# Local attention with a feed-forward gate: a reordered first quarter, and a planner that repairs modelled TensorE waits

## The chip, the cores and the metric

The kernel runs on one core of one Trainium2 chip. A core has five engines that run their own instruction streams side by side: TensorE (PE in the profile; its weight loads are listed as PEld), VectorE (DVE), ScalarE (ACT), GpSimd (POOL) and SyncE (SP), which issues most of the DMA transfers. The metric is the device time of one execution in microseconds; lower is better. It is given as the median of several runs.

## The reference

With x of 2048 tokens by 640 features, xn its layer norm, everything in float32:

```python
def _A_ref(x, wqkv, wo):          # x is xn here
    H = 32; Dh = D // H; W, dil = 8, 2
    qkv = (x @ wqkv).reshape(B, S, 3, H, Dh)          # q, k, v per head
    idx = pos[:, None] - (jnp.arange(W) * dil)[None, :]
    logits = einsum("bhsd,bhswd->bhsw", q, k[idx]) * Dh ** -0.5   # masked where idx < 0
    o = einsum("bhsw,bhswd->bhsd", softmax(logits), v[idx])
    return o.reshape(B, S, D) @ wo

def _B_ref(x, w1, w2):            # w1: 640 x 1536, w2: 1536 x 640
    return silu(x @ w1) @ w2

xn = layernorm(x)
return x + _A_ref(xn, wqkv, wo) * silu(_B_ref(xn, w1, w2))
```

Each token attends to eight tokens: itself and those 2, 4, ... 14 positions before it.

## The kernel before

**Groups and phases.** The 2048 tokens are cut into NG = 4 groups of 512 tokens, each of T = 4 tiles of 128. A group runs a q/k/v phase in NQ = 4 quarters of eight heads (480 columns of wqkv each), then the feed-forward phase with the output product of the group before woven in. The last output product ends the program.

**Two halves of every number.** Each float32 operand is split into a high part, rounded to TensorE's fast float32r format, and a residual low part. A product is three matmuls: high x high, low x high, high x low. For weights, line 479 (ACT) rounds a raw chunk into its high half `whi`, line 483 (GpSimd or VectorE) subtracts it from the raw chunk into the low half `wlo`, and for most chunks line 487 (SP) stores both for the later groups. For activations, TensorE transposes a piece, line 782 (ACT) copies it to `TH`, and line 786 (VectorE) subtracts into `TL`.

**The first quarter** (`first_quarter`, lines 745 to 838) is written out by hand, because nothing is loaded yet. TensorE first transposes the identity matrix WARM = 28 times, as dummy work (line 751). Each of the four token tiles is loaded into `XIN`, its statistics are taken by VectorE in two halves of 320 columns (line 764) and joined (765), ACT takes the root (526), VectorE the reciprocal (528), and VectorE normalizes it in two pieces (769). `PARTS` says how the five chunks of 128 columns are cut into the two pieces: three and two. `turn(t)` is the five transposes of tile t (778) with their copies (782) and residuals (786). `products(t, steps)` issues matmuls (799) for tile t; a step (k, c) is pass k on weight chunk c, with k = 0 high x high, 1 low x high, 2 high x low. A step (0, c) needs the rounded chunk, (2, c) its residual, (1, c) the activation's residual. The quarter has 4 tiles x 15 steps. The order of these calls is TensorE's order.

**Weight chunks in the first quarter.** The first RING = 7 chunks are loaded ahead (`raw_load`, 444 on SP, 440 on ACT for the chunk numbers in `BY_ACT`). Chunks 0 to 4 belong to the first quarter. Of the chunks below LO = 10, GpSimd subtracts the residual except for those in `ON_DVE`, (2, 3, 4), which VectorE does.

**The planner** (`Weave`). All work is first noted as operations with an engine, a modelled duration, keys that they read and write, and a priority. `order` then runs a model: each engine takes, among its operations whose inputs are there, the one that can start first, by priority among equals; TensorE keeps the order in which its work was noted. GpSimd's and VectorE's operations marked `lock` exclude each other in this model. The landing times of the first transfers are the constants `EARLY`, later ones follow a rate. The instructions are emitted in the order of their modelled starts. On the chip this fixes the order inside each engine and each DMA queue; between engines only real data dependences hold, by semaphores. So an order in the model between an operation of GpSimd and one of VectorE that share no data is not kept on the chip.

**Queues in the first microseconds.** SP issues the first half of tile 0, then chunk 0, tile 1 (`X_AT` = 3 for it, against priority 1 + k for chunk k), chunks 2, 3 and 4, tile 2, chunks 5 and 6, tile 3, and more chunks. ACT's queue takes the second half of tile 0 and chunk 1.

**The last quarter.** `o_rest` (730 to 742) transposes the last two chunks of the attention output of the last group (738, residual on VectorE at 742); VectorE's attention work before it is lines 680 to 720, its largest instructions being 680, 683 and 712.

Of the kernel before, what the change touches and what calls it, by code (L numbers as in the profile page):

```python
# [15 lines left out]
P = 128  # L16
# [40 lines left out]
TILE_AT = 1, 1.5, 5, 6  # L57
LOW_AT = 3
NOW = 3
ON_DVE = (2, 3, 4)  # L60


def win(ap, n, step):
# [10 lines left out]

class Op:
    __slots__ = ("eng", "dur", "fn", "prio", "lock", "table", "nbytes", "more", "late", "seq", "left", "users", "ready", "start", "end",
                 "spans")


class Weave:  # L80
# [19 lines left out]
    def add(self, eng, dur, fn, reads=(), writes=(), prio=0.0, lock=False, table=None, nbytes=0, more=0.0, late=0.0, at=0.0,  # L100
            spans=()):
        o = Op()
        o.eng, o.dur, o.fn, o.prio, o.lock, o.table, o.nbytes = eng, dur, fn, prio, lock, table, nbytes
        o.more, o.late, o.spans = more, late, spans
        o.seq, o.users, o.ready = len(self.ops), [], at
        before = set()
        for k in reads:
            if k in self.writer:
                before.add(self.writer[k])
        for k in writes:  # L110
            if k in self.writer:
                before.add(self.writer[k])
            before.update(self.readers.get(k, ()))
        for k in writes:
            self.writer[k] = o
            self.readers[k] = []
        for k in reads:
            self.readers.setdefault(k, []).append(o)
        before.discard(o)
        o.left = len(before)  # L120
        for b in before:
            b.users.append(o)
        self.ops.append(o)
        return o

    def order(self):
        engines = ("PE", "POOL", "DVE", "ACT", "SP")
        free = dict.fromkeys(engines, 0.0)
        can = {e: [] for e in engines}
        tensor = [o for o in self.ops if o.eng == "PE"]  # L130
        at = moved = 0
# [8 lines left out]
                        if a[0] == b[0] and a[1] < b[2] and b[1] < a[2] and (a[3] or b[3])), default=0.0)  # L140

        for o in self.ops:
            if o.left == 0:
                can[o.eng].append(o)
        done = []
        while len(done) < len(self.ops):
            best = None
            for e in engines:
                if e == "PE":
                    c = [tensor[at]] if at < len(tensor) and tensor[at].left == 0 else []  # L150
                else:
                    c = can[e]
                if not c:
                    continue
                f = free[e]
# [3 lines left out]
                if best is None or m < best[0] or (m == best[0] == lock and held == best[1].eng):  # L159
# [11 lines left out]
            o.start = t  # L171
            dur = o.dur
            if e == "ACT" and o.table is not None and o.table != table:
                table = o.table
# [2 lines left out]
            if o.nbytes:  # L177
                dma = max(dma, t + dur) + o.nbytes / self.RATE
                o.end = self.EARLY[moved] if moved < len(self.EARLY) else dma + self.LAND + o.more
                moved += 1  # L180
                lanes[e] = lanes[e][1:] + [o.end]
            else:
                o.end = t + dur
                if o.lock:
                    lock, held = o.end, e
            if e == "PE":
                at += 1
            else:
# [3 lines left out]
                live = [p for p in live if p.end > t - 30] + [o]  # L192
            for u in o.users:
                u.left -= 1
                u.ready = max(u.ready, o.end + (self.HOP + u.late if u.eng != e or o.nbytes else 0.0))
                if u.left == 0:
                    can[u.eng].append(u)
        self.span = max(o.end for o in done)
        return sorted(done, key=lambda o: (o.start, o.seq))

    def emit(self):
        for o in self.order():
            o.fn()


# [1 line left out]
def local_attention_silu_ffn(ctx: ExitStack, tc: tile.TileContext, x, wqkv, wo, w1, w2, out):  # L207
# [80 lines left out]
    po = lambda n: 0.11 + n * 0.0023  # L288

    def dve(n, fn, reads, writes, prio, lock=False, late=0.0, spans=()):  # L290
        add("DVE", dv(n), fn, reads, writes, prio, lock, late=late, spans=spans)

    def act(n, fn, reads, writes, prio, table=None, more=0.0, late=0.0, at=0.0, spans=()):
        add("ACT", ac(n) + more, fn, reads, writes, prio, table=table, late=late, at=at, spans=spans)

    def free_for(old, new):

# [95 lines left out]
        return QAT if i < first_q else 0  # L393

    raw_in = {}

    def raw_tile(k):

# [56 lines left out]
    def w_load():  # L455
# [19 lines left out]
        if not k:  # L475
            raw_load(0)
            rawn[0] = 1
        raw, kr = raws.pop(i)
        act(n, lambda: nc.scalar.activation(whi, raw, AF.Copy), kr + [("sd", 0)] * (k < 2), [kh], 1000 + due)
# [3 lines left out]
        add(eng, cost, lambda: by.tensor_tensor(out=wlo, in0=raw, in1=whi.bitcast(F32), op=OP.subtract),  # L483
            [kh] + kr + wait, [kl], due if pool_does else LOW_AT if k < LO else 50, lock=True)
# [38 lines left out]

    def ln_rstd(a, b, at=1):
        n = range(a, b)
        act(b - a, lambda: nc.scalar.activation(SD[:, 0, a:b], MV[:, a:b, 1], AF.Sqrt, bias=epst, scale=1.0),
            [("mv", t) for t in n], [("sd", t) for t in n], 0, "sqrt")
        dve(10, lambda: nc.vector.reciprocal(out=SD[:, 1, a:b], in_=SD[:, 0, a:b]),
            [("sd", t) for t in n], [("rs", t) for t in n], at)

    def ln_apply(t):
# [213 lines left out]
    def first_quarter(i):  # L745
# [3 lines left out]
        def warm(n, where):  # L749
            for k in range(n):  # L750
                nc.tensor.transpose(where[:, tsl(k % T)], ident, ident)
        pe(5.1, lambda: warm(WARM, ROT[0]), ["consts"], [("rot", 0)])

        PARTS = (0, 3), (3, DC)

        def begin(t):

# [2 lines left out]
            for k in range(2):  # L760
                cs = slice(k * 320, (k + 1) * 320)
                kx = ("xin", t) if t or k else ("xin", t, "a")
                turn_of = [("rs", t - 1)] if t == T - 1 else []
                dve(320, lambda k=k, cs=cs: nc.vector.bn_stats(out=st[:, k, :], in_=XIN[:, t, cs]), [kx] + turn_of, [ks + (k,)], at)  # L764
            dve(60, lambda: nc.vector.bn_aggr(out=MV[:, t, :], in_=st), [ks + (0,), ks + (1,)], [("mv", t)], -1)
            ln_rstd(t, t + 1, -1)
            for j, (a, b) in enumerate(PARTS):
                cs = slice(a * P, b * P)
                dve((b - a) * 64, lambda cs=cs: nc.vector.tensor_scalar(
                    out=XIN[:, t, cs], in0=XIN[:, t, cs], scalar1=MV[:, t, 0:1], scalar2=SD[:, 1, t:t + 1],  # L770
                    op0=OP.subtract, op1=OP.mult), [("rs", t), ("mv", t), ("xin", t)], [("xn", t, j)], at, lock=True)

        def turn(t):
# [5 lines left out]
                pe(0.11 * (b - a), go, [("xin", t), ("xn", t, j)], [kp])  # L779
            for a, b, j, tp, kp in parts:  # L780
                v = tp[:, :(b - a) * P].rearrange("p (c n) -> p c n", n=P)
                act((b - a) * P, lambda a=a, b=b, v=v: nc.scalar.activation(TH[i][:, a:b, tsl(t)], v, AF.Copy),
                    [kp], t_keys(i, range(a, b), [t], ["th"]), 0)
            for a, b, j, tp, kp in parts:
                v = tp[:, :(b - a) * P].rearrange("p (c n) -> p c n", n=P)
                dve((b - a) * P, lambda a=a, b=b, v=v: nc.vector.tensor_tensor(
                    out=TL[i][:, a:b, tsl(t)], in0=v, in1=TH[i][:, a:b, tsl(t)].bitcast(F32), op=OP.subtract),
                    [kp] + t_keys(i, range(a, b), [t], ["th"]), t_keys(i, range(a, b), [t], ["tl"]), 0)

# [46 lines left out]
        wv.writer["first"] = wv.ops[-1]  # L836
        w_done(DC)
        return ps
# [327 lines left out]
```

## Time and profile before

| | us |
|---|---|
| median of 3 runs | 627.77 (627.76 to 629.12) |
| the profiled execution: its span, first to last instruction | 625.9 |
| TensorE busy | 620.5 |
| VectorE busy | 543.9 |
| ScalarE busy | 264.6 |
| GpSimd busy | 110.8 |
| moved by DMA | 166 MB, mean 265 GB/s |

The profiled execution gives its span; the times of the runs also hold what lies around the span. "L799" is line 799 of the kernel. A row of the time line has the start, the length, the engine, the line, the operation, what it writes and reads, and the count of instructions merged in the row; in brackets stands the idle time before it and what ended it. TensorE's matmuls overlap, and their ends are modelled, so the distance of two starts says more than a matmul's length. A row of "groups by form" ends with busy us in total, mean ns of one instruction, and the idle time before them.

### The profile page before, as it was taken

How to read it: one execution, taken by the hardware profiler on the slowest of the kernel's cores; microseconds unless marked ns; L12 is line 12 of the kernel's file. 1: busy time of each engine (PE TensorE's matmuls, PEld its weight loads, DVE VectorE, ACT ScalarE, POOL GpSimd, SP SyncE). 2: the span in 40 equal slices, each digit the busy share in tenths (PEclk: the TensorE clock that was granted, in tenths of full speed). 3: DMA queues.
4: the chain of work that ended last, by engine and by line, in shares of the span. 5: the costliest groups of instructions: out<-in, count | busy, mean ns of one | idle time of the engine just before them, and what ended most of it. 6: DMA issues, size and time to landing. Idle time of an engine off the chain costs nothing.

```text
span 625.9 us, 9040 instructions
## 1 busy us (share of the span) xinstructions
PE 620.5 (99%) x3423; PEld 560.8 (90%) x3423; DVE 543.9 (87%) x548; ACT 264.6 (42%) x490; POOL 110.8 (18%) x159
## 2 busy tenths in 40 slices
PE   8999999999999999999999999999999999999997
PEld 7888899998889999999888998999988999999997
DVE  6599999999788988999969999999754999998934
ACT  5435556363536316353434504445644343252220
POOL 4500000011110142112221115211222211111100
PEclk9999999999999999999999999999999999999999
DMA  9999999499999999994899999999999999887662
GB/s 295 319 309 318 319 397 343 165 315 300 278 321 300 302 214 308 291 221 135 207 275 277 316 354 233 316 155 284 219 225 280 241 329 228 278 225 238 203 190 85
DMA packets 99260, 166.07 MB, mean 265 GB/s; under 512 B 31008, under 2 KB 60672, under 8 KB 99216
## 3 DMA queue, kind: packets, MB, share of 16 engines
q1 hardware_dynamic: 72720, 85.77, 53.1%
q0 software_dynamic: 25952, 79.31, 46.4%
q8 instruction: 27, 0.44, 0.3%
q10 hardware_dynamic: 544, 0.41, 0.2%
q14 instruction: 17, 0.14, 0.1%
HBM read 107.91 MB, written 34.16 MB: 227 GB/s over the span
## 4 chain that ended last, share of the span: by engine, by line
PE 98%; DMA 1%; DVE 0%; SPq 0%; issue 0%
PE acc L912 22%; PE acc L914 15%; PE acc L874 10%; PE acc L873 10%; PE acc L872 10%; PE rot L1038 9%; PE rot L1037 9%; PE rot L1036 9%; PE acc L799 2%; PE rot L542 1%; DMA xin<-in_A_x_dram 1%; PE rot L1022 0%; PE rot L778 0%; PE rot L738 0%; DVE st L764 0%; SPq L444 0%
## 5 line engine op out<-in xcount | busy, mean ns | idle before, releaser
L912 PE MATMUL acc<-w,sh 128*128 128x384 f32 x384 | 113.2, 334 | 0.0
L872 PE MATMUL acc<-w,th 128*128 128x512 f32 (+2 forms) x300 | 113.2, 377 | 0.0
L874 PE MATMUL acc<-w,th 128*128 128x512 f32 (+2 forms) x300 | 112.9, 376 | 0.0
L873 PE MATMUL acc<-w,tl 128*128 128x512 f32 (+2 forms) x300 | 112.8, 376 | 0.0
L914 PE MATMUL acc<-w,sh 128*128 128x256 f32 x384 | 107.1, 279 | 0.0
L680 DVE TENSOR_TENSOR pr<-q,kv 128x2560 f32<-128x2560 f32 x32 | 90.2, 2819 | 13.9 <-DMA kv<-kv 13.7
L1049 ACT ACTIVATE sh<-rot 128x512 fp32r<-128x512 f32 x48 | 28.8, 599 | 155.8 <-PE rot L1038 155.7
L1036 PE MATMUL rot<-th,w 128*128 128x512 f32 x240 | 94.4, 393 | 0.0
L1037 PE MATMUL rot<-tl,w 128*128 128x512 f32 x240 | 93.8, 391 | 0.0
L1038 PE MATMUL rot<-th,w 128*128 128x512 f32 x240 | 93.8, 391 | 0.0
L712 DVE TENSOR_TENSOR pr<-q,kv 128x2560 f32<-128x2560 f32 x32 | 90.3, 2822 | 0.7
L683 DVE TENSOR_REDUCE l<-pr 128x128 f32<-128x2560 f32 x32 | 90.0, 2813 | 0.2
L470 POOL DMA_DIRECT2D w<-half_q x52 | 37.4, 719 | 233.4 <-DMA xr<-in_A_wqkv_dram 93.0
L717 DVE TENSOR_TENSOR pr<-pr 128x1280 f32<-128x1280 f32 x64 | 75.4, 1179 | 1.3
L470 POOL DMA_DIRECT2D w<-half_w x72 | 38.6, 537 | 213.5 <-PE acc L914 98.2
L914 PEld LDWEIGHTS acc<-w,sh 128*128 128x128 f32 x384 | 72.2, 188 | 1.0
L912 PEld LDWEIGHTS acc<-w,sh 128*128 128x128 f32 x384 | 72.1, 188 | 1.0
L874 PEld LDWEIGHTS acc<-w,th 128*128 128x128 f32 x300 | 56.3, 188 | 8.7
L873 PEld LDWEIGHTS acc<-w,tl 128*128 128x128 f32 x300 | 56.3, 188 | 8.7
L872 PEld LDWEIGHTS acc<-w,th 128*128 128x128 f32 x300 | 56.3, 188 | 8.6
L912 PE MATMUL acc<-w,sl 128*128 128x384 f32 x192 | 57.8, 332 | 0.0
L639 ACT ACTIVATE kv<-acc 128x320 f32<-128x320 f32 x64 | 28.2, 440 | 68.7 <-PE acc L874 66.4
(115 smaller groups left out, 1036.0 us busy)
## 6 DMA issues: line engine op xcount, KB each, us to landing
w<-half_w POOLq DMA_DIRECT2D x72, 640.0 KB, 8.6
w<-half_q POOLq DMA_DIRECT2D x39, 512.0 KB, 5.6
half_w<-w SPq DMA_DIRECT2D x24, 640.0 KB
kv<-kv SPq DMA_DIRECT2D x16, 560.0 KB
kv<-kv SPq DMA_DIRECT2D x16, 420.0 KB
w<-half_wo POOLq DMA_DIRECT2D x10, 640.0 KB, 6.8
gate<-in_B_w_dram SPq DMA_DIRECT2D x16, 320.0 KB
w<-half_q POOLq DMA_DIRECT2D x13, 384.0 KB, 8.6
```

The source lines that it names most:

```text
L470: add("POOL", 1.0, lambda: nc.gpsimd.dma_start(both, src), [("half", u), ("half", u, "more")], [kh, kl], due + 10, nbytes=2 * n * P * 4)
L680: dve(2560, lambda t=t: nc.vector.tensor_tensor(out=PR, in0=win(qq[:, t:t + 2, :], W, 0), in1=win(kv[:, 0, t:t + 2, :], W, CQ), op=OP.mult ...
L683: dve(2560, lambda t=t: nc.vector.tensor_reduce(out=l[:, t:t + 2].rearrange("p t w h -> p (t w h)"), in_=PR.rearrange("p t w (h d) -> p (t ...
L712: dve(2560, lambda t=t, v=v: nc.vector.tensor_tensor(out=PR.rearrange("p t w (h d) -> p t (w h) d", d=DH), in0=e[:, t:t + 2].rearrange("p ...
L872: nc.tensor.matmul(o, hi, wh, start=c == 0, stop=False)
L873: nc.tensor.matmul(o, lo, wh, start=False, stop=False)
L874: nc.tensor.matmul(o, hi, wl, start=False, stop=c == DC - 1)
L912: nc.tensor.matmul(a[t][0][:, :CA], st, w[:, :CA], start=first, stop=last)
L914: nc.tensor.matmul(b[t // 2][0][:, h * CB:(h + 1) * CB], st, w[:, CA:], start=first and h == 0, stop=last, skip_group_check=True)
L1036: nc.tensor.matmul(h, wh[:, cs], TH[i][:, c, :], start=c == 0, stop=False)
L1037: nc.tensor.matmul(h, wh[:, cs], TL[i][:, c, :], start=False, stop=False)
L1038: nc.tensor.matmul(h, wl[:, cs], TH[i][:, c, :], start=False, stop=c == DC - 1)
```

## The change

*Constants.* WARM goes from 28 to 20. The first steps of tile 0 get a new order, with (2, 0) as the second. Chunk 0 in place of chunk 1 is loaded on ACT's queue; tile 1's load moves up to priority 1.2, ahead of chunk 1. `EARLY` gets other landing times. `ON_DVE` is gone, so GpSimd subtracts all ten residuals. `PARTS` becomes two chunks and three. The steps of the four tiles are interleaved in a new order, with tile 0's and tile 1's last (2, c) steps put later.

*Fixed orders.* `chain` makes each of a list of operations a predecessor of the next in the model. One list orders VectorE's work of the first quarter (statistics `st`, aggregate `ag`, reciprocal `rc`, normalization `ap`, residual `tl`, each with tile and piece), one ACT's (`sq` the root, `hi` the rounding of a chunk, `th` the copy of a transposed piece), and one puts GpSimd's residuals `lo` and three of VectorE's normalizations in turn.

*The repair.* `plan` runs the model, takes the first modelled wait of TensorE over 0.03 after model time 6, follows back what made it late (`blame`: operations that stood behind another one on their engine), tries for each such pair to put the late one first, keeps the one that moves the waiting TensorE work furthest forward, and goes on, up to 90 trials in all.

```diff
-WARM, WARM2 = 28, 3
+WARM, WARM2 = 20, 3
-FIRST = (0, 0), (0, 1), (1, 0), (1, 1), (0, 2), (1, 2), (0, 3), (1, 3), (0, 4), (1, 4)
-BY_ACT = (1,)
+FIRST = (0, 0), (2, 0), (1, 0), (0, 1), (1, 1), (0, 2), (1, 2)
+ON_VECTOR = (("st", 0, 0), ("st", 0, 1), ("ag", 0), ("rc", 0), ("ap", 0, 0), ("ap", 0, 1), ("st", 1, 0), ("st", 1, 1), ("tl", 0, 0),
+             ("ag", 1), ("tl", 0, 1), ("rc", 1), ("ap", 1, 0), ("ap", 1, 1), ("st", 2, 0), ("tl", 1, 0), ("tl", 1, 1), ("st", 2, 1),
+             ("ag", 2), ("rc", 2), ("ap", 2, 0), ("ap", 2, 1), ("st", 3, 0), ("st", 3, 1), ("tl", 2, 0), ("ag", 3), ("tl", 2, 1),
+             ("rc", 3), ("ap", 3, 0), ("ap", 3, 1))
+ON_SCALAR = (("sq", 0), ("hi", 0), ("th", 0, 0), ("th", 0, 1), ("hi", 1), ("sq", 1), ("hi", 2), ("hi", 3), ("th", 1, 0), ("th", 1, 1),
+             ("hi", 4))
+BY_ACT = (0,)
-X_AT = 3, 6, 8
+X_AT = 1.2, 6, 8
-LOW_AT = 3
-NOW = 3
-ON_DVE = (2, 3, 4)
...
-    EARLY = 3.9, 3.8, 4.9, 5.3, 6.05, 6.95, 7.7, 8.4, 9.4
+    EARLY = 4.1, 3.9, 5.5, 5.2, 6.5, 7.3, 8.1, 8.85, 9.7
+    TRIES = 90
...
+    def chain(self, *ops):
+        for a, b in zip(ops, ops[1:]):
+            a.users.append(b)
+            b.need += 1
...
+    def blame(self, o):
+        pairs, todo, seen = [], [(o, 0)], set()
+        while todo:
+            o, depth = todo.pop()
+            if o is None or o in seen or depth > 12 or (o.eng == "PE" and depth):
+                continue
+            seen.add(o)
+            b = o.behind
+            if o.eng != "PE" and b is not None and o.start > o.ready + 1e-6 and b.end > o.ready or o.nbytes and b is not None:
+                if b.eng != "PE":
+                    pairs.append((o, b))
+                todo.append((b, depth + 1))
+            if not (o.eng != "PE" and o.start > o.ready + 1e-6):
+                todo.append((o.why, depth + 1))
+        return pairs
...
+    def plan(self):
+        tensor = [o for o in self.ops if o.eng == "PE"]
+        self.next = {a: [b] for a, b in zip(tensor, tensor[1:])}
+        done = self.order()
+        left, given_up = self.TRIES, set()
+        while left > 0:
+            gap = next((o for o in self.gaps(done) if o not in given_up), None)
+            if gap is None:
+                break
+            was, found = gap.start, None
+            for a, b in self.blame(gap):
+                if self.reaches(b, a):
+                    continue
+                a.users.append(b)
+                b.need += 1
+                self.order()
+                left -= 1
+                a.users.pop()
+                b.need -= 1
+                if gap.start < was - 0.02 and (found is None or (gap.start, self.span) < found[:2]):
+                    found = gap.start, self.span, a, b
+            if found is None:
+                given_up.add(gap)
+            else:
+                self.chain(*found[2:])
+            done = self.order()
+        return done
...
     def emit(self):
-        for o in self.order():
+        for o in self.plan():
...
-        pool_does = k < LO and k not in ON_DVE
+        pool_does = k < LO
...
-        pe(5.1, lambda: warm(WARM, ROT[0]), ["consts"], [("rot", 0)])
-        PARTS = (0, 3), (3, DC)
+        pe(4.9, lambda: warm(WARM, ROT[0]), ["consts"], [("rot", 0)])
+        PARTS = (0, 2), (2, DC)
...
         products(0, FIRST)
         turn(1)
-        products(0, [(2, c) for c in range(NOW)])
-        products(1, passes(0, 1))
-        products(0, [(2, c) for c in range(NOW, DC)])
+        products(0, [(0, 3), (1, 3)])
+        products(1, [(0, 0), (0, 1), (0, 2), (0, 3), (1, 0), (1, 1)])
+        products(0, [(0, 4), (1, 4), (2, 1)])
+        products(1, [(0, 4), (1, 2), (1, 3), (1, 4), (2, 0), (2, 1)])
         turn(2)
-        products(1, passes(2))
+        for t in range(2):
+            products(t, [(2, 2)])
         products(2, passes(0, 1))
         turn(3)
-        products(2, passes(2))
+        for t in range(3):
+            products(t, [(2, 3)])
+        products(2, [(2, c) for c in range(3)])
+        for t in range(3):
+            products(t, [(2, 4)])
         products(3, passes(0, 1, 2))
+        wv.chain(*(head[k] for k in ON_VECTOR))
+        wv.chain(*(head[k] for k in ON_SCALAR))
+        wv.chain(head["lo", 0], head["ap", 1, 1], head["lo", 1], head["lo", 2], head["ap", 2, 1], head["lo", 3], head["ap", 3, 1],
+                 *(head["lo", k] for k in range(4, RING)))
```

More of the change, by code (lines that the diff above doesn't have):

```diff
@@ L76 @@
     __slots__ = ("eng", "dur", "fn", "prio", "lock", "table", "nbytes", "more", "late", "seq", "left", "users", "ready", "start", "end",
-                 "spans")
+                 "spans", "need", "at", "why", "behind")
 class Weave:
@@ L104, in add @@
         o.more, o.late, o.spans = more, late, spans
-        o.seq, o.users, o.ready = len(self.ops), [], at
+        o.seq, o.users, o.at, o.need = len(self.ops), [], at, 0
         before = set()
@@ L119, in add @@
         before.discard(o)
-        o.left = len(before)
+        self.ops.append(o)
         for b in before:
-            b.users.append(o)
-        self.ops.append(o)
-        return o
+            self.chain(b, o)
+        return o
+    def chain(self, *ops):
+        for a, b in zip(ops, ops[1:]):
+            a.users.append(b)
+            b.need += 1
     def order(self):
@@ L128, in order @@
         free = dict.fromkeys(engines, 0.0)
+        last = dict.fromkeys(engines)
         can = {e: [] for e in engines}
@@ L142, in order @@
         for o in self.ops:
+            o.left, o.ready, o.why = o.need, o.at, None
             if o.left == 0:
@@ L158, in order @@
                 m = min(est)
-                if best is None or m < best[0] or (m == best[0] == lock and held == best[1].eng):
+                if best is None or m < best[0] or (m == best[0] == lock and held is not None and held.eng == best[1].eng):
                     pick = min((o for o, t in zip(c, est) if t <= m + 1e-9), key=lambda o: (o.prio, o.seq))
@@ L171, in order @@
             o.start = t
+            o.behind = held if o.lock and held and held.end > free[e] else last[e]
+            last[e] = o
             dur = o.dur
@@ L184, in order @@
                 if o.lock:
-                    lock, held = o.end, e
+                    lock, held = o.end, o
             if e == "PE":
@@ L194, in order @@
                 u.left -= 1
-                u.ready = max(u.ready, o.end + (self.HOP + u.late if u.eng != e or o.nbytes else 0.0))
+                when = o.end + (self.HOP + u.late if u.eng != e or o.nbytes else 0.0)
+                if when > u.ready:
+                    u.ready, u.why = when, o
                 if u.left == 0:
@@ L199, in order, with reaches @@
         return sorted(done, key=lambda o: (o.start, o.seq))
+    def reaches(self, a, b):
+        seen, todo = {a}, [a]
+        while todo:
+            o = todo.pop()
+            if o is b:
+                return True
+            for u in o.users + self.next.get(o, []):
+                if u not in seen:
+                    seen.add(u)
+                    todo.append(u)
+        return False
+    def blame(self, o):
+        pairs, todo, seen = [], [(o, 0)], set()
+        while todo:
+            o, depth = todo.pop()
[10 more added lines that the diff above has]
+        return pairs
@@ new lines, in gaps @@
+    def gaps(self, done):
+        end = 0.0
+        for o in done:
+            if o.eng == "PE":
+                if o.start > max(end, self.FROM) + 0.03:
+                    yield o
+                end = o.end
+    FROM = 6.0
+    def plan(self):
[25 more added lines that the diff above has]
+        return done
@@ L290, in dve @@
     def dve(n, fn, reads, writes, prio, lock=False, late=0.0, spans=()):
-        add("DVE", dv(n), fn, reads, writes, prio, lock, late=late, spans=spans)
+        return add("DVE", dv(n), fn, reads, writes, prio, lock, late=late, spans=spans)
     def act(n, fn, reads, writes, prio, table=None, more=0.0, late=0.0, at=0.0, spans=()):
-        add("ACT", ac(n) + more, fn, reads, writes, prio, table=table, late=late, at=at, spans=spans)
+        return add("ACT", ac(n) + more, fn, reads, writes, prio, table=table, late=late, at=at, spans=spans)
     def free_for(old, new):
@@ L395, in local_attention_silu_ffn @@
     raw_in = {}
+    head = {}
     def raw_tile(k):
@@ L478, in w_load @@
         raw, kr = raws.pop(i)
-        act(n, lambda: nc.scalar.activation(whi, raw, AF.Copy), kr + [("sd", 0)] * (k < 2), [kh], 1000 + due)
-        pool_does = k < LO and k not in ON_DVE
+        head["hi", k] = act(n, lambda: nc.scalar.activation(whi, raw, AF.Copy), kr + [("sd", 0)] * (k < 2), [kh], 1000 + due)
+        pool_does = k < LO
         eng, cost, by = ("POOL", po(n), nc.gpsimd) if pool_does else ("DVE", dv(n), nc.vector)
         wait = [("xn", 0, 1)] if pool_does and k < DC else []
-        add(eng, cost, lambda: by.tensor_tensor(out=wlo, in0=raw, in1=whi.bitcast(F32), op=OP.subtract),
-            [kh] + kr + wait, [kl], due if pool_does else LOW_AT if k < LO else 50, lock=True)
+        head["lo", k] = add(eng, cost, lambda: by.tensor_tensor(out=wlo, in0=raw, in1=whi.bitcast(F32), op=OP.subtract),
+            [kh] + kr + wait, [kl], due if pool_does else 50, lock=True)
         if what[i] == "store":
```

14 lines of the change are left out of this document (7 added, 7 removed).

## The prediction

> **What bounds the kernel now.** First the page: span, busy time, and the engines' shares of the chain that ended last.
>
> ```profile
> span 625.9 us, 9040 instructions
> PE 620.5 (99%) x3423; PEld 560.8 (90%) x3423; DVE 543.9 (87%) x548; ACT 264.6 (42%) x490; POOL 110.8 (18%) x159
> PE 98%; DMA 1%; DVE 0%; SPq 0%; issue 0%
> ```
>
> TensorE is the bound. The profiled execution spans 625.9; the median of the runs shown is 627.77, so 1.9 lie around the span and I carry them unchanged. Next, where TensorE is not busy (windows: length, then busy time of PE, PEld, DVE, ACT, POOL, clock, DMA), and the list of what PE waited for:
>
> ```profile
> 6.85:23.40 16.55, 16.36 (x85) 13.27 (x84) 10.85 (x29) 10.21 (x27) 5.36 (x5) 1.00 1.09 368
> 23.40:590.00 566.60, 566.60 (x3099) 511.16 (x3099) 514.03 (x477) 245.84 (x448) 101.26 (x145) 1.00 1.04 271
> 590.00:600.00 10.00, 9.98 (x62) 9.01 (x62) 7.64 (x11) 3.37 (x6) 1.59 (x3) 1.00 0.60 198
> 622.00:625.90 3.90, 0.11 (x1) 0.00 (x0) 0.85 (x2) 0.00 (x0) 0.00 (x0) 0.76 0.24 84
> ...
> PE rot L751 <- POOL ident masks.py:199: 1.4, 1, 1.4
> ```
>
> From 23.4 to 590 there is no idle time at all, and 0.02 in the ten us behind. So repairing modelled TensorE waits there has nothing to win: the waits that the planner sees are not on the chip. What is left is the first 23.4 us and the 3.8 after the last matmul, which the diff does not touch. A matmul's end is modelled, so inside the first quarter I count starts, not busy time:
>
> ```profile
> 6.85 0.71 PE L778 MATMUL rot<-ident,xin 128*128 128x128 f32 x5
> 7.92 0.70 PE L799 MATMUL acc<-w,th 128*128 128x480 f32 x2
> ...
> 13.26 1.24 PE L799 MATMUL acc<-w,tl 128*128 128x480 f32 x5
> 14.78 0.71 PE L778 MATMUL rot<-ident,xin 128*128 128x128 f32 x5
> 15.24 2.41 PE L799 MATMUL acc<-w,th 128*128 128x480 f32 x10
> 17.49 1.24 PE L799 MATMUL acc<-w,tl 128*128 128x480 f32 x5
> ...
> 22.35 1.24 PE L799 MATMUL acc<-w,th 128*128 128x480 f32 x5
> 23.43 0.38 PE L872 MATMUL acc<-w,th 128*128 128x480 f32 x1
> L751 PE MATMUL rot<-ident x22: 421/421/476, 1.4 to 5.9; 128*128 128x128 f32 x22
> L751 PE MATMUL rot<-ident x28: 272/421/476, 1.4 to 6.7; 128*128 128x128 f32 x28
> ```
>
> A product costs (23.43-22.35)/5 = 0.216, a transpose (17.49-14.78-10x0.216)/5 = 0.11. The quarter has 60 products, 20 transposes and 3 dummies: 12.96+2.2+0.33 = 15.5. It takes 23.43-6.85 = 16.6, so 1.1 are waits, nearly all before 13.3: from there 42 products and 10 transposes need 9.07+1.1 = 10.17 and take 10.17. Ahead of it, 22 dummies start at 1.4 to 5.9, one per 4.5/21 = 0.214, at 421 ns; the last six come faster, at 272: the clock went up near 6.1.
>
> **The change, part by part.** These rows carry the prices (time line, then groups by form: busy, mean ns):
>
> ```profile
> 1.21 0.70 SPq L444 DMA_DIRECT2D pr<-in_A_wqkv_dram  x1
> 3.74 0.89 DVE L764 BATCH_NORM_STATS2 st<-xin 128x6 f32<-128x320 f32 x2 [2.29 <-DMA xin<-in_A_x_dram]
> 5.43 0.80 DVE L769 TENSOR_SCALAR xin<-xin,mv,sd 128x384 f32<-128x384 f32 x2
> 6.27 1.10 ACT L479 ACTIVATE w<-pr 128x480 fp32r<-128x480 f32 x2 [1.07 <-DMA pr<-in_A_wqkv_dram]
> 6.96 2.40 POOL L483 TENSOR_TENSOR w<-pr,w 128x480 fp32r<-128x480 f32 x2 [3.73 <-ACT w L479]
> 7.14 0.89 DVE L764 BATCH_NORM_STATS2 st<-xin 128x6 f32<-128x320 f32 x2 [0.91 <-DMA xin<-in_A_x_dram]
> 8.51 1.58 ACT L479 ACTIVATE w<-pr 128x480 fp32r<-128x480 f32 x3
> 9.04 0.86 DVE L769 TENSOR_SCALAR xin<-xin,mv,sd 128x384 f32<-128x384 f32 x2
> 9.82 1.78 DVE L483 TENSOR_TENSOR w<-pr,w 128x480 fp32r<-128x480 f32 x3
> 11.03 0.61 ACT L479 ACTIVATE w<-xr 128x480 fp32r<-128x480 f32 x1 [0.94 <-DMA xr<-in_A_wqkv_dram]
> 11.53 0.48 DVE L764 BATCH_NORM_STATS2 st<-xin 128x6 f32<-128x320 f32 x1
> 21.73 1.59 ACT L479 ACTIVATE w<-gate 128x480 fp32r<-128x480 f32 x3 [0.71 <-issue]
> ...
> L786 DVE TENSOR_TENSOR tl<-rot,th 128x384 fp32r<-128x384 f32 x4 | 2.2, 545 | 2.0 <-ACT th L782 1.9
> L769 DVE TENSOR_SCALAR xin<-xin,mv,sd 128x384 f32<-128x384 f32 x4 | 2.0, 492 | 0.1
> L786 DVE TENSOR_TENSOR tl<-rot,th 128x256 fp32r<-128x256 f32 x4 | 1.6, 410 | 0.0
> L769 DVE TENSOR_SCALAR xin<-xin,mv,sd 128x256 f32<-128x256 f32 x4 | 1.6, 405 | 0.0
> L765 DVE BATCH_NORM_AGGREGATE mv<-st 128x2 f32<-128x12 f32 x4 | 0.8, 209 | 0.1
> L526 ACT ACTIVATE sd<-mv,epst 128x1 f32<-128x1 f32 x4 | 1.2, 300 | 2.5 <-DVE mv L765 2.5
> L528 DVE RECIPROCAL sd<-sd 128x1 f32<-128x1 f32 x4 | 0.6, 162 | 0.7 <-ACT sd L526 0.7
> ```
>
> *Eight dummies fewer.* The 20th starts at 1.4+19x0.214 = 5.5 and is out of the way at 5.7. Tile 0's first normalized piece, now two chunks, is ready at 5.43+0.41 = 5.84. So the first transpose starts near 5.95 instead of 6.85: 0.9 gained, if what follows keeps up. Nothing else needed the dummies but the clock (a rival below).
>
> *Loads.* Weight chunk 0 goes to ACT's queue, which held chunk 1; on SP tile 1 moves up past one weight issue of 0.70, and chunk 1 falls behind it. Chunk 0 lands between 3.74 (tile 0, ahead of it on its queue) and 6.27 (its consumer now). I take 5.8, nearer the late end because tile 1 now shares the transfers with it. Its rounding (0.6) ends at 6.45, then come the copies of tile 0's transposes, then the first product near 7.05 instead of 7.92. The fixed order of ACT adds a wait here: both copies stand behind chunk 0's rounding, and PE behind them.
>
> *(2,0) as second product* waits for GpSimd: 6.45+1.2 = 7.7. All of PE stands behind it, with some 0.5 of the 0.9 lost again; but what is late next decides anyway.
>
> *Tile 1.* It lands between 6.27 (chunk 0, which held its place on SP) and 7.14; I take 6.5. Behind it on DVE: statistics 0.89, the first residual 0.41, aggregate 0.21, residual 0.55, reciprocal 0.16, both normalizations 0.9 less 0.1 of overlap: 9.5. Three transposes later, 9.9, PE has six products that need no more: 9.9+6x0.216 = 11.2.
>
> *Tile 2* must pass its first statistics on DVE before tile 1's first residual: in the fixed order of DVE, 0.48+0.41 after it lands. It lands after chunk 4 (the third of the three at 8.51, so by 9.5) and before the chunk rounded at 11.03, which stands behind it on SP: bounds 9.5 and 11.03, giving 10.4 to 11.9 for the residual; I take the middle, 11.2. Before, 11.53 came from DVE's three weight subtractions (1.78), which now go to GpSimd.
>
> *The rest of the quarter* from 11.2: 47 products and 10 transposes, 10.15+1.1 = 11.25, so it ends at 22.45. Tile 2's normalization is due on PE 11 products later, 13.6; DVE needs 0.55+0.48+0.21+0.3+0.16+0.8 = 2.5 and is done at 13.7: 0.1 lost. End 22.55 against 23.43: 0.9 gained. With tile 2's bounds, 0.2 to 1.4 (where tile 1 decides no later).
>
> *GpSimd.* All weight residuals of the quarter go there, 1.2 each, and the order "residual, normalization, residual" exists only in the planner: nothing on the chip makes GpSimd wait for DVE. The pair of normalizations at 9.04 ran beside GpSimd until 9.36 and took 0.86, against 0.80 for the pair at 5.43 without it. From that row a blocked pair costs 0.06; the other end is one residual, 1.2. I take 0.3 in all, nearer the row.
>
> The Trainium skill (SBUF — State Buffer, section "SBUF: two separate sides") says that GpSimd and a two-port DVE instruction hold one port pair by an exclusive lock, for the whole instruction. By that, the first normalization at 9.04 would have begun at 9.36 and the pair ended at 10.16; it ended at 9.90, so the row bears the rule out at most in part.
>
> *SP.* The stores of chunks 2 to 4 wait for GpSimd now, up to 2 us later, with the raw loads of the second quarter behind them on SP; those are rounded from 21.7 on, so this is covered. The planner's repairs after the quarter change orders on DVE, ACT, POOL and SP: taken as 0.
>
> Sum: -0.9+0.3 = -0.6; span 625.3, time 627.2.
>
> **The rivals.** *All waits go:* 5.95+15.5 = 21.45, 2.0 gained: 625.8. Against it: chunk and tile landings set the waits, and their order only shifts. *The loads land no earlier:* tile 1 at 7.14 makes 11.8, tile 2 late as well: 0.3 gained and lost to GpSimd, 627.8. For it: the three landings at 6.27, 7.14 and 11.03 follow each other under a full DMA (share 1.09). *GpSimd gets in front of both normalizations of tile 1:* 2x1.2 on the path that ends at 9.5, less 0.5 of slack against tile 2: -0.9+1.9 = +1.0, 628.8. That is the lock of the Trainium skill's SBUF — State Buffer at work, which the row at 9.04 shows at most in part.
>
> *The last quarter* is the one on the slower side. There DVE, not PE, is nearly late:
>
> ```profile
> L742 DVE TENSOR_TENSOR tl<-rot,th x2: 691/692/692, 594.6 to 596.6; 128x512 fp32r<-128x512 f32 x2
>   PEld rot L738: 0.4, 1
> L712 DVE TENSOR_TENSOR pr<-q,kv x32: 2812/2824/2827, 66.9 to 587.8; 128x2560 f32<-128x2560 f32 x32
> ```
>
> PE's transposes at L738 already wait for DVE's L742. If a repair puts one 2.82 product in front of what L742 needs, all of it falls on PE: 627.2+2.8 = 630.0. It decides as soon as DVE is over 0.02 later than now. Against it: a repair is kept only where the planner's own next wait moves forward.
>
> *The clock stays low.* If the shorter run of dummies kept PE at half rate for another stretch like 1.4 to 6.1 (4.7), some 4 us of work between 6 and 10.8 would take 8, with 1 us of waits to absorb it: +3, 630.2. Against it: transposes follow the dummies 0.25 later. The Trainium skill (TensorE: Matmul & The Clock Gate, part 1) has a free-running window of about 3.4 us of sustained activity; with that in place of 4.7 the price would be about 2, an estimate. The trace agrees as far as it goes: 4.7 from the first dummy to the faster pace lies between one such window and two.
>
> **How the numbers follow.** Forecast (gain of 0.2 to 1.4) 0.52; loads no earlier 0.15; GpSimd 0.14; all waits gone 0.06; last quarter 0.09; clock 0.04. The measurement of this kernel tells 0.3%, 1.9 us, from no change. Only "all waits gone" reaches that bound on the fast side: faster 0.06. The last two and the tail of GpSimd's make slower 0.14. The rest, 0.80, is same. The forecast's own range is 626.4 (1.4 gained, nothing lost to GpSimd) to 627.9 (0.2 gained); the range to 8 in 10 takes in the loads and GpSimd: 625.8 to 629.4.
>
> **What would show it.** First real transpose near 5.95; first product near 7; tile 1's first statistics before 7.14; the first L872 near 22.5; no PE wait from there to 590. Wrong if the first L872 is later than 23.4, if a normalization in the quarter takes over 1 us, or if PE shows waits after the quarter.

## The result and the profile after

| kernel | median us | runs | span of the profiled execution |
|---|---|---|---|
| before | 627.82 (627.58 to 629.12) | 8 | 625.9 |
| changed | 629.61 (629.28 to 630.71) | 8 | 627.5 |

The changed kernel takes 1.0028 of the time before, with a 95% interval of 1.0018 to 1.0038: 1.8 us slower, 0.2 above the upper end of the predicted range. Here and below, medians and ratios leave out the few runs in the chip's slower state, and a ratio is not that of the two medians shown, because it also weighs some runs of before of 630 to 636 us (for e5, further down, the medians alone give 0.9985, the ratio 0.9958).

The page of the changed kernel, span, busy time and the chain that ended last:

```profile
span 627.5 us, 9020 instructions
PE 620.1 (99%) x3415; PEld 559.4 (89%) x3415; DVE 548.2 (87%) x545; ACT 264.9 (42%) x490; POOL 116.2 (19%) x162
PE 97%; DVE 1%; ACT 1%; DMA 0%; issue 0%
```

The windows that were shown of before (length, then busy time of PE, PEld, DVE, ACT, POOL, clock, DMA), and what PE waited for:

```profile
6.85:23.40 16.55, 14.63 (x71) 11.18 (x70) 13.71 (x31) 8.54 (x23) 7.95 (x7) 1.00 0.96 305
23.40:590.00 566.60, 566.60 (x3099) 511.13 (x3098) 513.30 (x471) 247.38 (x451) 103.45 (x145) 1.00 1.01 272
590.00:600.00 10.00, 9.98 (x59) 8.76 (x58) 8.02 (x9) 2.69 (x5) 1.20 (x3) 1.00 0.68 217
...
PE rot L863 <- DVE xin L854: 1.9, 3, 0.8
```

Behind the first quarter all is as before: from its end to the end of the span it is 602.6 us, against 602.5 (625.9-23.43). Inside it TensorE now idles 1.92 of 16.55 us where it was 0.19, and it waits for VectorE's normalization (L854, which was L769). The time line of PE in the first quarter of the changed kernel:

```profile
5.91 0.94 PE L863 MATMUL rot<-ident,xin 128*128 128x128 f32 x5 [0.19 <-DVE xin L854]
6.92 1.07 PE L884 MATMUL acc<-w,th 128*128 128x480 f32 x2
...
9.37 0.44 PE L863 MATMUL rot<-ident,xin 128*128 128x128 f32 x2
10.64 0.55 PE L863 MATMUL rot<-ident,xin 128*128 128x128 f32 x3 [0.84 <-DVE xin L854]
...
14.91 0.44 PE L863 MATMUL rot<-ident,xin 128*128 128x128 f32 x2
16.19 0.55 PE L863 MATMUL rot<-ident,xin 128*128 128x128 f32 x3 [0.84 <-DVE xin L854]
...
24.92 0.38 PE L967 MATMUL acc<-w,th 128*128 128x480 f32 x1
```

The start came as predicted: first transpose 5.91, first product 6.92, 0.9 and 1.0 earlier. Then, in tile 1 and again in tile 2, two transposes run and the other three stand 1.27 and 1.28 after them. The quarter ends at 24.92 instead of 23.43: 1.5 later, of the 1.6 by which the span grew. What VectorE and GpSimd did at the first of these places, single instructions of the changed kernel:

```profile
7.94 1.23 POOL L568 TENSOR_TENSOR w<-pr,w 128x480 fp32r<-128x480 f32 x1 [0.48 <-ACT w L564]
8.28 1.04 DVE L854 TENSOR_SCALAR xin<-xin,mv,sd 128x256 f32<-128x256 f32 x1
9.12 1.25 POOL L568 TENSOR_TENSOR w<-pr,w 128x480 fp32r<-128x480 f32 x1
9.24 1.35 DVE L854 TENSOR_SCALAR xin<-xin,mv,sd 128x384 f32<-128x384 f32 x1
10.33 1.33 POOL L568 TENSOR_TENSOR w<-pr,w 128x480 fp32r<-128x480 f32 x1
10.51 0.48 DVE L849 BATCH_NORM_STATS2 st<-xin 128x6 f32<-128x320 f32 x1
10.91 0.40 DVE L871 TENSOR_TENSOR tl<-rot,th 128x256 fp32r<-128x256 f32 x1
```

Each normalization starts on time and its row only grows longer; no idle time is shown. The first ends at 9.32, 0.15 after the GpSimd residual that was running (7.94+1.23 = 9.17). By then GpSimd's next residual is under way, and the second normalization ends at 10.59, 0.22 after that one (9.12+1.25 = 10.37). The statistics at 10.51 and the residual from PSUM at 10.91 run beside GpSimd at their usual 0.48 and 0.40. So it is not VectorE as a whole that GpSimd holds up, but the normalization. Tile 2 repeats it:

```profile
13.48 2.44 POOL L568 TENSOR_TENSOR w<-xr,w 128x480 fp32r<-128x480 f32 x2
...
13.62 2.52 DVE L854 TENSOR_SCALAR xin<-xin,mv,sd 128x256 f32<-128x256 f32 x2
```

The pair takes 2.52 and ends at 16.14, 0.22 after GpSimd's second (15.92). The planner's order, "residual, normalization, residual", holds in its model alone. On the chip GpSimd runs its residuals as soon as their chunks are rounded.

### The profile page after: what moved, and what is told of

Same layout as the page of the kernel before. It is cut to its first block, busy times and chain, and to the rows that moved or that the text cites. A ratio compares the mean times of both kernels' runs of the same rounds, so it can differ in the third digit from the quotient of the medians.

```text
span 627.5 us, 9020 instructions
## 1 busy us (share of the span) xinstructions
PE 620.1 (99%) x3415; PEld 559.4 (89%) x3415; DVE 548.2 (87%) x545; ACT 264.9 (42%) x490; POOL 116.2 (19%) x162
## 4 chain that ended last, share of the span: by engine, by line
PE 97%; DVE 1%; ACT 1%; DMA 0%; issue 0%
PE acc L1007 22%; PE acc L1009 15%; PE acc L969 10%; PE acc L968 10%; PE acc L967 10%; PE rot L1132 9%; PE rot L1133 9%; PE rot L1131 9%; PE acc L884 1%; PE rot L627 1%; DVE xin L854 1%; DMA xin<-in_A_x_dram 0%; PE rot L863 0%; ACT w L564 0%; PE rot L1117 0%; PE rot L823 0%
## 5 line engine op out<-in xcount | busy, mean ns | idle before, releaser
L802 DVE TENSOR_TENSOR pr<-pr 128x1280 f32<-128x1280 f32 x64 | 77.1, 1205 | 1.4
```

The lines of the kernel that those rows point to most:

```text
L802: dve(2 * n * CQ, lambda n=n: nc.vector.tensor_tensor(out=PR[:, :, 0:n, :], in0=PR[:, :, 0:n, :], in1=PR[:, :, n:2 * n, :], op=OP.add), [] ...
```

## The experiments

The times of before are those measured on the same chip beside each kernel.

| run | what it is | median us | before | ratio, 95% interval |
|---|---|---|---|---|
| e1 | changed, GpSimd held | 630.16 | 627.59 | 1.0038, 1.0015 to 1.0060 |
| e2 | changed, no repair | 633.92 | 627.59 | 1.0090, 1.0066 to 1.0114 |
| e3 | before, all residuals on GpSimd | 632.41 | 627.59 | 1.0065, 1.0018 to 1.0112 |
| e4 | before, repair alone | 628.16 | 627.59 | 1.0017, 0.9983 to 1.0052 |
| e5 | as e1, its tile last in SBUF | 626.81 | 627.74 | 0.9958, 0.9924 to 0.9992 |
| e6 | before, four unused bytes | 630.82 | 627.74 | 1.0048, 1.0019 to 1.0077 |
| e7 | e5 with 28 dummies | 630.98 | 627.74 | 1.0040, 1.0011 to 1.0069 |
| e8 | e5 with the loads of before | 632.02 | 627.74 | 1.0050, 1.0022 to 1.0078 |
| e9 | as e7, orders of e5 | 627.07 | 627.84 | 0.9977, 0.9954 to 1.0000 |
| e10 | changed, three residuals back on VectorE | 634.44 | 627.84 | 1.0095, 1.0061 to 1.0129 |

**e1: the planner's order made real.** A one-column sum on GpSimd reads the end of a normalized tile, so that GpSimd really waits for it.

```diff
     epst, SD = small("epst", 1), small("sd", 2, T)
+    HELD = small("held", 1)
...
+        for t, k in ((1, 1), (2, 3), (3, 4)):
+            last = XIN[:, t, D - 1:D]
+            o = add("POOL", po(1), lambda last=last: nc.gpsimd.tensor_tensor(out=HELD, in0=last, in1=last, op=OP.add),
+                    [("xn", t, 1), ("xin", t)], [("held",)], 0)
+            wv.chain(head["ap", t, 1], o, head["lo", k])
         wv.writer["first"] = wv.ops[-1]
```

> Changed kernel, with GpSimd made to wait on the chip for what only the planner's order says: a one-column sum of tile 1, 2 and 3 after their second normalization stands in front of the residuals of chunks 1, 3 and 4. Theory (GpSimd's residuals stood in front of four normalizations, 1.0 us lost for tile 1 and 1.0 for tile 2): the pairs of normalizations take 0.8 to 0.9 instead of 2.31 and 2.52, the quarter ends near 22.9 instead of 24.92, time 629.6 - 2.0 = 627.6. Rival (the repairs, the loads or the missing dummies cost the time): the pairs get short, but the time stays over 629.

The quarter did what the theory says: it ended at 22.38, 2.5 before the changed kernel, and no normalization took over 0.48. The time did not follow, 630.16: over 629, as the rival had it, though for none of its reasons, as e5 and e6 will show. No row shows a new wait of TensorE. Between 23 and 620 us the products themselves had become slower. Products of line 912 (here L1013) in the groups by form, busy us and mean ns, of before, then of e1:

```profile
L912 PE MATMUL acc<-w,sh 128*128 128x384 f32 x384 | 113.2, 334 | 0.0
```

```profile
22.38 0.38 PE L973 MATMUL acc<-w,th 128*128 128x480 f32 x1
...
L1013 PE MATMUL acc<-w,sh 128*128 128x384 f32 x384 | 115.2, 338 | 0.0
```

The 384-column products from sl went the same way, from a mean of 332 to 338, and those of 256 columns from 279 to 280.

The tile for the sum, four bytes per partition, stood ahead of the tiles sh, sl and others, so the addresses behind it had moved. That became a theory of its own, for e5 and e6.

**e2: the changed kernel without the repair.**

```diff
-        for o in self.plan():
+        for o in self.order():
```

> Changed kernel without the repair: the planner's first order is emitted. Theory: the repair has no part in the loss; the quarter ends between 24.5 and 25.3, no TensorE wait behind it, time 629.2 to 630.0. Rival (the repair's swaps made the loss): 627.8 or below.

633.92, against the theory and against its rival. The loss in the quarter is the same (it ended at 25.03, and PE waited 2.2 for L854), so the repair did not make it. But without the repair three waits stand later that neither before nor the changed kernel has. PE's waits in e2:

```profile
PE rot L863 <- DVE xin L854: 2.2, 3, 0.8
PE acc L1007 <- DVE sl L1146: 1.4, 1, 1.4
...
PE rot L823 <- DVE o L805: 1.3, 1, 1.3
PE acc L967 <- ACT gate L1220: 1.1, 1, 1.1
```

These three add up to 3.8 of the 4.3 between this kernel and the changed one. The new first quarter shifts the plan of all that follows, the planner's first order of it is late at three places, and the repair mends all three.

**e3: more GpSimd residuals in the kernel before.**

```diff
-ON_DVE = (2, 3, 4)
+ON_DVE = ()
```

> Kernel before with one edit: the residuals of chunks 2, 3 and 4 go to GpSimd as well. Theory: GpSimd runs five residuals back to back from 7.0 to 13.2, so two to four normalizations of tiles 1 and 2 last 1.0 to 1.4 instead of 0.4 to 0.5, and the first quarter ends 0.5 to 2 later: 628.3 to 629.8. Rival (the port is not the cause): 627.8, or faster, because VectorE has 1.8 less to do.

The theory's mark is there, one normalization of 1.36 and a wait of 2.0 behind it, but the time is far over its range. The five residuals of GpSimd, that normalization, the waits, and a window of e3:

```profile
6.97 6.06 POOL L483 TENSOR_TENSOR w<-pr,w 128x480 fp32r<-128x480 f32 x5 [3.74 <-ACT w L479]
...
11.82 1.36 DVE L769 TENSOR_SCALAR xin<-xin,mv,sd 128x256 f32<-128x256 f32 x1
...
PE rot L1036 <- DMA w<-half_w: 2.8, 1, 2.8
PE rot L778 <- DVE xin L769: 2.0, 1, 2.0
PE rot L738 <- DVE o L720: 1.3, 1, 1.3
...
13.90:17.20 3.30, 3.30 (x9) 2.66 (x9) 2.73 (x9) 0.49 (x2) 1.52 (x2) 0.50 1.10 383
```

GpSimd ended at 13.03 and this normalization, one of 256 columns, at 13.18: again 0.15 later. The wait of 2.0 was followed by a stretch at half clock (0.50), nine matmuls in 3.3 us, and the other plan brought two later waits, 2.8 and 1.3. The quarter ended at 27.00, 3.6 later than before. One edit, four prices: only the first was in the expectation.

**e4: the repair alone on the kernel before** (its `plan`, `blame` and `chain`, landing constants as before).

> Kernel before with the repair alone, first quarter and landing constants as before. Theory: TensorE's waits in the model are not on the chip; 627.8 within 0.4. Rival (the repairs shift work on VectorE that TensorE needs): over 628.5, with new waits of TensorE in the profile.

628.16, the interval holds 1: no gain to be seen. A small loss is likely, for all ten runs (from 627.78) lie above the median of before, and the rival's mark is there in small. TensorE waits 0.3 for tile 1's second normalization, which now starts at 11.16, behind a weight residual of VectorE at 10.59; in the kernel before the two normalizations ran as a pair. The quarter ended 0.4 later than before, at 23.80:

```profile
23.80 0.38 PE L953 MATMUL acc<-w,th 128*128 128x480 f32 x1
```

**e5: e1 with the tile behind all others.**

```diff
-    HELD = small("held", 1)
...
     TURN = sb.tile([P, TOK], F32, name="turn")
+    HELD = small("held", 1)
```

> As the held kernel (GpSimd really waits for tiles 1, 2 and 3), but the one-column tile lies behind all others in SBUF instead of ahead of the operand tiles. Theory (the first quarter gained 2.4 us there against the changed kernel, and the shifted addresses of the operand tiles gave 3.1 back through slower products): no shift now, the first quarter ends near 22.5, the mean of the 128x384 products from sh is 334 again, time 627.6 - 0.8 = 626.8, between 626.3 and 627.3. Rival (the drift came from the wait itself or from the later schedule): 630 again.

As the theory has it: 626.81, 0.9 below before. Against the changed kernel that is 2.7, each taken against before on its own chip. It is the fastest of all here, and its slowest run (627.12) is faster than the fastest run of before beside it (627.22). Its normalizations (x8 is their count; then shortest, median and longest ns), GpSimd's wait, and the end of the quarter:

```profile
L855 DVE TENSOR_SCALAR xin<-xin,mv,sd x8: 411/444/476, 5.6 to 16.2; 128x256 f32<-128x256 f32 x4, 128x384 f32<-128x384 f32 x4
...
9.73 0.19 POOL L934 TENSOR_TENSOR held<-xin 128x1 f32<-128x1 f32 x1 [2.17 <-DVE xin L855]
9.88 2.40 POOL L569 TENSOR_TENSOR w<-pr,w 128x480 fp32r<-128x480 f32 x2
...
22.83 0.38 PE L973 MATMUL acc<-w,th 128*128 128x480 f32 x1
```

No normalization is over 476 ns. GpSimd idles 2.17 and starts after the pair. The quarter ends 2.1 before that of the changed kernel, and what follows it takes 602.5, as before.

**e6: nothing but four bytes.**

```diff
     epst, SD = small("epst", 1), small("sd", 2, T)
+    PAD = small("pad", 1)
```

> Kernel before with one edit: an unused tile of four bytes per partition where the held kernel had its own, ahead of sh, sl and what follows. Theory (addresses): the first quarter is as before, the mean of the 128x384 products from sh goes from 334 to 338, time 627.6 + 3.1 = 630.7. Rival (addresses play no part): 627.6.

630.82: an unused tile in the kernel before costs 3.1, with the same group means as in e1 (busy us, mean ns; the 256-column group has 280 again). The first quarter, which ended at 23.27, has no part in it:

```profile
L913 PE MATMUL acc<-w,sh 128*128 128x384 f32 x384 | 115.2, 338 | 0.0
```

Which of the shifted tiles matters, and to which multiple it has to lie, was not tried.

**e7 and e9: the dummies.** Both are e5 with WARM = 28. In e7 the planner also counts them as 28 (5.1), in e9 as 20 (4.9), so that the other engines run e5's orders unchanged.

> The held kernel (tile last) with 28 dummy transposes instead of 20. Theory: the first real transpose is back at 6.85, 0.9 later; of that, what tile 1's chain does not absorb shows at the end of the quarter: 0.2 to 0.9 over the held kernel, 627.0 to 627.7. Rival (the dummies are worth nothing, tile 1 decides): as the held kernel.

> The held kernel (tile last) with 28 dummy transposes, but with the modelled time of 20, so that VectorE, ScalarE, GpSimd and SyncE run exactly the instructions of the held kernel in its order. Theory (the loss of the run with 28 dummies came from another order in the last quarter, not from the dummies; the start of the clock hides most of what dummies cost): no wait of TensorE near 594, 626.5 to 627.4. Rival (28 dummies cost what they take): 0.9 over the held kernel or more, and over 630 if the last quarter's wait came from them.

627.07 in e9: the eight dummies cost 0.3 in the medians (626.81 to 627.07), or 0.2 when each is set against before on its own chip. In e7 the same TensorE work takes 630.98, for 0.2 of modelled time. Its windows and its PE near the end:

```profile
594.00:598.30 4.30, 1.04 (x7) 0.80 (x7) 3.33 (x5) 0.15 (x1) 0.00 (x0) 1.00 0.42 143
598.40:601.70 3.30, 3.30 (x9) 2.57 (x8) 2.16 (x3) 0.37 (x2) 0.00 (x0) 0.50 0.58 177
601.90:610.00 8.10, 8.10 (x57) 8.10 (x56) 2.16 (x3) 3.73 (x8) 0.53 (x1) 1.00 0.57 204
...
597.46 0.66 PE L824 MATMUL rot<-ident,o 128*128 128x128 f32 x4 [3.26 <-DVE o L806]
```

TensorE stands 3.3 for the last attention output, and then runs some 3.3 us at half clock. This is the last quarter's rival of the prediction, at its place: VectorE's order there is another one, and TensorE pays all of it. The dummies in e7 and in e9:

```profile
1.37 4.75 PE L837 MATMUL rot<-ident 128*128 128x128 f32 x28 [1.37 <-POOL ident masks.py:199]
```

```profile
1.38 5.71 PE L837 MATMUL rot<-ident 128*128 128x128 f32 x28 [1.38 <-POOL ident masks.py:199]
```

The same 28 took 4.75 in one execution and 5.71 in the other, as TensorE's pace rose sooner or later: in e7 four matmuls lie in the half us up to 4.5 and seven in the next, in e9 seven only from 6.5. e1 and e5, whose orders are the same, end their quarters at 22.38 and 22.83. So quarter ends of two single profiles compare to about half a us, no better.

**e8: the loads.** e5 with BY_ACT = (1,), X_AT = 3, 6, 8 and the old EARLY.

> The held kernel (tile last) with the loads as before: chunk 1 on ACT's queue, tile 1 behind chunk 0 on SP, old landing constants. Theory: chunk 0 lands at 6.27 instead of 5.55 and tile 1 at 7.14 instead of 6.15, so the quarter ends 0.5 to 1.0 later: 627.3 to 627.8. Rival (tile 2 decides the quarter, its landing is unchanged): as the held kernel.

The time, 632.02, says nothing of the loads: this plan too has the wait of 3.3 for the last attention output. The quarter, before it, ended at 23.33, 0.5 after e5's. Chunk 0 and tile 1 came at 6.59 and 7.48 (time line, then the wait):

```profile
6.59 0.60 ACT L565 ACTIVATE w<-pr 128x480 fp32r<-128x480 f32 x1 [1.51 <-DMA pr<-in_A_wqkv_dram]
7.48 0.89 DVE L850 BATCH_NORM_STATS2 st<-xin 128x6 f32<-128x320 f32 x2 [1.36 <-DMA xin<-in_A_x_dram]
...
23.33 0.38 PE L973 MATMUL acc<-w,th 128*128 128x480 f32 x1
...
PE rot L824 <- DVE o L806: 3.3, 1, 3.3
```

That is the lower end of the theory's 0.5 to 1.0, but no more than the half us by which single profiles differ, so it does not decide against the rival.

**e10: the changed kernel with the residuals of chunks 2, 3 and 4 on VectorE.**

```diff
-        pool_does = k < LO
+        pool_does = k < LO and k not in (2, 3, 4)
...
-            [kh] + kr + wait, [kl], due if pool_does else 50, lock=True)
+            [kh] + kr + wait, [kl], due if pool_does else 3 if k < LO else 50, lock=True)
```

> Changed kernel with one part undone: the residuals of chunks 2, 3 and 4 are VectorE's again. Theory: the residual of chunk 1 still stands in front of tile 1's first normalization (0.9 lost), but nothing stands in front of its second one, and tile 2's are hit at most by chunks 5 and 6: the quarter ends 0.5 to 1.5 before the changed kernel's 24.92, and if the planner's new order brings no wait later, 628.1 to 629.1. Rival (who subtracts plays no part): 629.6.

The quarter ended at 23.56, 1.4 before the changed kernel's, as expected; the time, 634.44, did not follow. The residuals of chunks 5 and 6 still meet tile 2: its first normalization, of 256 columns, took 1.40 and ended at 14.38, 0.15 after GpSimd. Its first product behind the quarter, and its waits of PE:

```profile
23.56 0.38 PE L967 MATMUL acc<-w,th 128*128 128x480 f32 x1
...
PE rot L823 <- DVE o L805: 2.8, 1, 2.8
...
PE acc L967 <- DMA w<-half_q: 1.0, 1, 1.0
...
PE rot L1131 <- ACT sf L1145: 0.5, 1, 0.5
```

A third plan, and again the last quarter is late, by 2.8. In the profiled execution (632.73) the three later waits add 4.3 to a quarter that is 1.4 better.

## Why the prediction was wrong

*What bounds the kernel*: right. The loss came from the first quarter alone, and the changed kernel has no new wait behind it.

*Dummies, loads, tiles 1 and 2*: right as a sum. First transpose 5.91 (5.95 forecast), first product 6.92 (7.05), tile 1's first statistics 6.15 (6.5), the residual behind tile 2's 10.91 (11.2). With GpSimd held, the quarter ends at 22.83 (22.55 forecast), 0.6 sooner than before in these two profiles, and the median is 0.9 below before: the term of -0.9 has its size. Its parts are less sure. The eight dummies alone are worth 0.2 to 0.3 (e9), and what the loads and the new order of steps are worth was not timed apart. The 1.4 at the upper end of the gain follows from no sum shown: with tile 1 as it was taken, PE has work until 11.2, so that an earlier tile 2 gains nothing more. The rounding of chunk 0 ends at 6.4 by its own terms (5.8+0.6), not 6.45; neither slip decided anything.

*GpSimd* is the step that failed: "From that row a blocked pair costs 0.06; the other end is one residual, 1.2. I take 0.3 in all, nearer the row." The step was forecast at +0.3. Held, as in e5, the quarter ends 2.1 sooner, the profiled span is 2.2 shorter (625.3), and the time 2.7 lower, so the term is 2.1 to 2.7. (Of the changed kernel the fastest run was profiled, of e5 the slowest, so the spans differ by less than the medians.) The sign that the prediction named for being wrong, a normalization of over 1 us, is there four times (1.04, 1.35, 1.24 and 1.35). The row was misread. These are its instructions, in the kernel before:

```profile
8.13 1.23 POOL L483 TENSOR_TENSOR w<-pr,w 128x480 fp32r<-128x480 f32 x1
...
9.04 0.54 DVE L769 TENSOR_SCALAR xin<-xin,mv,sd 128x384 f32<-128x384 f32 x1
```

GpSimd ended at 9.36, the normalization at 9.58: 0.22 later, the very distance of the 384-column ones in the changed kernel. It was blocked there too. A free one of that form takes 0.49, of which only the last 0.22 have to follow GpSimd, so an overlap of 0.32 stretched it by hardly more than 0.05. The cost is not the overlap; it is GpSimd's end plus 0.15 (256 columns) or 0.22 (384) where that is later than the normalization's own end. The other end of that bound, one residual of 1.2, was too low as well. Each of four normalizations stood behind a residual of its own, because GpSimd's next one gets in between the two of a pair: the pairs took 1.5 and 1.7 longer than 0.80.

The prediction weighed the lock of the Trainium skill (SBUF — State Buffer, section "SBUF: two separate sides") against that same row and held that the row bore it out at most in part. That an instruction of GpSimd which has started keeps the normalization out until its end is what the changed kernel's trace shows: 9.32 behind 9.17, 10.59 behind 10.37. The other way round, a normalization that holds up GpSimd, no row here shows clearly; in e10 one that started at 12.98 still had to wait for a residual that started at 13.01. That page of the Trainium skill limits the lock to VectorE instructions in a two-port mode or with two SBUF inputs, and the unslowed 0.48 and 0.40 rows agree. That the mode of the normalization is the reason was not tried.

*The rival "GpSimd gets in front of both normalizations of tile 1"* had the mechanism and its sign, at a chance of 0.14. Its price, 628.8, was for tile 1 alone. Tile 2 was hit the same way, with the residuals of chunks 5 and 6.

*The repair, "taken as 0"*, was right against before only as a balance: it gains nothing on the old plan (e4), and it takes back some 4.3 that the new quarter's plan loses without it (e2). "Repairing modelled TensorE waits there has nothing to win" held for the plan in the profile, not for the plan that the change makes.

*The last quarter* did not decide the changed kernel, but five of the ten experiments show its wait: 1.3 in e2 and e3, 2.8 in e10, over 3 in e7 and e8. How a plan comes to it was not followed back. The 2.8 at which it was priced is of that size. *The clock* did not stay low in the changed kernel: three products there start at 7.83, 8.05 and 8.27, 0.22 apart, the full pace of the kernel before.

## What to carry to other kernels

An order that a planner sets between two engines is only a wish unless data or a semaphore carries it; look in the trace whether the second engine waited. An instruction that another engine blocked showed no idle time here: compare its length with its own free form, and its end with the other engine's end. Two kernels whose operand tiles lie at other addresses, or whose plan came out of a search run anew, differ by more than the edit; hold both still before a difference of 0.5% is read as its effect.

## What the runs showed of the hardware

- Four unused bytes per partition ahead of the operand tiles cost 3.1 us of 627.7 (e6): no wait behind the first quarter, but 128x384 products at a mean of 338 instead of 334 ns and more of the like.
- A wait of TensorE of 3.3 us (e7) or 2.0 us (e3) was followed by 3.3 us or more at a granted clock of 0.50; in e7 the windows on both sides, up to 598.30 and from 601.90, stand at 1.00. The Trainium skill (TensorE: Matmul & The Clock Gate, part 1) gives a window of about 3.4 us for the gate; between 3.3 and 3.6 in e7 agrees with it. The length of the wait does not decide alone: the waits of 2.8 us in e10 and e3, and those of 1.1 to 1.4 us in e2, were followed by a clock of 1.00. Runs of e7, whose orders are the same, differ likewise: five have a mean clock of 0.999 and took 629.93 to 630.67, five have 0.994 to 0.997 and took 631.30 to 634.07.
- The time for which the same 28 dummies ran differed by 1.0 between executions (4.75 in e7 and 5.71 in e9), as the faster pace began near 4.5 in the one and near 6.5 in the other. The granted clock reads 1.00 in all these windows, so this rise is seen in the pace alone.
